# Attention with a computed bias: keys and values loaded between the first groups of bias rows, and the later rows shifted where they are written to memory

## The chip, the cores and the metric

One core of one Trainium2 chip. The metric is the device time of one execution in microseconds (us), median of three runs.

## What is computed

Two batches, eight heads, 576 positions, head dimension 64, all in float32. The scores are the scaled products of queries and keys plus a bias that a small network computes from the distance of two positions; then a softmax, the product with the values, and two feed-forward blocks on the 1152 x 512 result.

```
scores = scale * np.matmul(q, k.transpose(0, 1, 3, 2))
psi_rel = np.log1p(np.abs(rel));  psi_i = np.log1p(np.maximum(pos[:, None], 1.0))
h = np.maximum((psi_rel / psi_i)[..., None] @ w1 + b1, 0.0)
scores = scores + (h @ w2).transpose(2, 0, 1)[None]
attn = softmax(scores);  x = np.matmul(attn, v)
x = swiglu_block(rms_norm(x));  out = (s * relu(x @ w_in) ** 2 + b) @ w_out
```

## The kernel before

The order of the work is written out by hand: each engine, and each engine's queue of transfers, runs its instructions in program order. SP (SyncE) issues all transfers named here. A transfer that it issues waits on SP for its data, and holds up those behind it.

**Bias.** The 576 query positions are cut into 36 groups of 16 (`g`), each with 16 x 8 heads = 128 rows. `hidden(g)` (L169) makes four tiles `hq`, one for each quad of queries, mostly on VectorE (L182), the third of some early groups on ScalarE (L178), the fourth on GpSimd from group 12 on. `bias_mm(g)` multiplies them with `w2` (L202), `bias_out(g)` (L206) moves the result out of PSUM into a tile `br` (four buffers), on ScalarE (L221), for group 20 on VectorE (L219). For groups 0 to 7 the row has all 576 columns already, and one transfer puts the 128 rows into the bias tile of chunk 0 (L229, `bias<-br`): partition 8 i + g of it takes query i's eight heads. From group 8 on a row has 591 columns, is the same for all 16 queries but for a shift, and makes a detour: it is written to DRAM as it stands (L225, `rows<-br`, row pitch 592), and `bias_in(g)` (L231) reads it back with another start for each query (L239, `bias<-rows`):

```
src = bass.AP(tensor=r.tensor, offset=r.offset + 15, ap=[[H * RW - 1, 16], [RW, H], [1, S]])
```

A chunk of bias is 128 queries, made of eight groups; two chunk buffers are in use. The last chunk has 64 queries, each group of it read back twice.

**Attention.** A unit `u` is a pair of heads of a tile of 128 queries (four units to a tile, the first four with batch 0, the next four with batch 1; 36 units). `scores_mm(u)` (L261) needs q of the tile and k number u % 8; `soft(u, e)` (L273, VectorE) adds the bias chunk, finds the extreme for the softmax and frees the PSUM bank of the scores; `expo` (L280, ScalarE); `turn_mm` (L289, L291) transposes, `turn_out` (L298) copies; `values_mm` (L339) needs v number u % 8. `finish_*` normalise a finished tile: `finish_n` (L380, `x`), `finish_c` (L386).

**The schedule.** Stage -2 makes groups 0 to 7, `hide(g + LEAD)` behind each (`groups`, L503). The loop `for s in range(-2, PAIRED)` then takes one unit a step: loads, group s + 11 (stage -1: groups 8 to 10 behind the first scores), `bias_in`, scores and `soft` of unit s + 1, `values_mm` of unit s - 1. In it k number s + 3 is loaded in steps -1 to 4, and v number s + 1 in steps 0 to 6; k 0, k 1 and v 0 come ahead of everything. From s = 8 on the loop `for s in range(PAIRED, NU + 2, 2)` takes two units a step, with `hide(s + 13)` and `hide(s + 14)` behind the second `expo`. All behind unit 35 (feed-forward blocks, weights split on ScalarE, VectorE and GpSimd) is untouched by the change.

Of the kernel before, what the change touches and what calls it, by code (L numbers as in the profile page):

```python
# [8 lines left out]
F32 = mybir.dt.float32  # L9
# [8 lines left out]
P = 128  # L18
B, H, S, D = 2, 8, 576, 64
# [10 lines left out]
NJ = 3  # L30
TJ = NT // NJ
RW = S + 16
NEAR = S + P
TILES = list(range(NTT))
POOL_QUAD = 3
# [10 lines left out]
PAIRED = 8  # L46
# [6 lines left out]
def tile_kernel(ctx: ExitStack, tc: tile.TileContext, q, k, v, ltab, lg, cst, cst2, rms_g, wg, wv, wo, win, wo2, s_p, b_p, out):  # L53
    nc = tc.nc
    ctx.enter_context(tc.manual_schedule())

    def pool(stack, name, bufs, side="left", space=None):
        kw = {"space": space} if space else {}
        return stack.enter_context(tc.tile_pool(name=name, bufs=bufs, side=side, reuse_waits="tile", **kw))
# [32 lines left out]
    dram = pool(att, "dram", 1, space=bass.MemoryType.DRAM)  # L92
# [4 lines left out]

    near = tab_p.tile([P, NEAR], F32, name="near")
    tab = tab_p.tile([P, S], F32, name="tab")
# [6 lines left out]
    cb = ac.tile([P, 2], F32, name="cb")  # L106
    spot = ac.tile([P, 1], F32, name="spot")
    owed = []
    g_row = tab_p.tile([1, DM + P], F32, name="g_row")
    mh = const.tile([P, 1], F32, name="mh")  # L110
    g_bc = const.tile([P, DM], F32, name="g_bc")
# [23 lines left out]
    def load_k(n):  # L135
        ks[n] = ac.tile([P, S], F32, name=f"ks{n}")
        nc.sync.dma_start(out=ks[n], in_=k[:, n])

    def load_v(n):
        t = ac.tile([P, 10, D], F32, name=f"vs{n}")  # L140
        nc.sync.dma_start(out=t, in_=v[:, n])
        vs[n] = t
# [21 lines left out]
    rows = {}  # L164

    def reach(g):
        return S if g < 8 else max(16 * g + 15, S - 1 - 16 * g) + 1

    def hidden(g, owed):  # L169
        hms[g] = []  # L170
        d = reach(g)
        for tq in range(4):
            n = 4 * g + tq
            hq = h_p.tile([P, S], F32, name="hq")[:, :d]
            src = near[:, P - 1 - 4 * n:P - 1 - 4 * n + S] if g < 8 else tab[:, :d]
            hms[g].append(hq)
            if tq == ACT_QUAD and g in ACT_EARLY:
                nc.scalar.activation(hq, src, AF.Relu, bias=nthr[:, n:n + 1], scale=w1_sb)  # L178
                continue

            def go(eng, hq=hq, src=src, n=n):
                eng.tensor_scalar(hq, src, w1_sb, thr[:, n:n + 1], op0=ALU.mult, op1=ALU.max)  # L182

            if tq != POOL_QUAD or g < POOL_FROM:
                go(nc.vector)
            elif owed is None:
                go(nc.gpsimd)
            else:
                owed.append(lambda go=go: go(nc.gpsimd))
# [16 lines left out]
    def bias_out(g, pb):  # L206
        left = 0 if g < 8 else 16 * g + 15
        br = br_p.tile([P, RW], F32, name="br")
        to = left + S - (16 * g if left else 0)
        if left:  # L210
            parts = [(br[:, left:to], pb[0][:, :to - left])]
            for f, bank in enumerate(pb):
                a, b = max(512 * f, 1), min(512 * f + 511, left)
                parts.append((br[:, left - b:left - a + 1], bank[:, b - 512 * f:(a - 512 * f - 1) if a > 512 * f else None:-1]))
        else:
            parts = [(br[:, :to], pb[:, :to])]
        for dst, src in parts:
            if g == PAIRED + 12:
                nc.vector.tensor_scalar(dst, src, minv_sb[:, g:g + 1], cb[:, 0:1], op0=ALU.mult, op1=ALU.add)  # L219
                continue  # L220
            nc.scalar.activation(dst, src, AF.Identity, bias=cb[:, 1:2] if g in ACT_EARLY else cb[:, 0:1],  # L221
                                 scale=minv_sb[:, g:g + 1])
        if left:
            rows[g] = dram.tile([P, RW], F32, name=f"rows{g}")
            nc.sync.dma_start(out=rows[g][:, :to], in_=br[:, :to])  # L225
        else:
            if 0 not in bias:
                bias[0] = bias_p.tile([P, H, S], F32, name="bias")
            nc.sync.dma_start(out=bias[0][g:P:8, :, :], in_=br[:, :to])  # L229

    def bias_in(g):  # L231
        qc, g16 = divmod(g, 8)
        if qc not in bias:
            bias[qc] = bias_p.tile([P, H, S], F32, name="bias")
        r = rows.pop(g)
        src = bass.AP(tensor=r.tensor, offset=r.offset + 15, ap=[[H * RW - 1, 16], [RW, H], [1, S]])
        for dst in ([0] if qc < 4 else [0, 64]):
            to = dst + (P if qc < 4 else D)
            nc.sync.dma_start(out=bias[qc][dst + g16:to:8 if qc < 4 else 4, :, :], in_=src)  # L239
# [25 lines left out]
    def soft(u, e, ps):  # L265
        if u % 4 == 0 and e == 0:
            sums[u // 4] = st_p.tile([P, H], F32, name="rs")
        if e == 0:
            prs[u] = pr_p.tile([P, 2 * S], F32, name="pr")
        h = 2 * (u % 4) + e  # L270
        sn = sn_p.tile([P, S], F32, name="sn")
        nm = st_p.tile([P, 1], F32, name="nm")
        nc.vector.tensor_tensor_reduce(out=sn, in0=ps, in1=bias[chunk(u)][:, h, :],  # L273
                                       scale=-1.0 / SCALE, scalar=3.0e38, op0=ALU.add, op1=ALU.min, accum_out=nm)
        sns[u, e] = sn, nm
# [179 lines left out]
    for g in range(AHD, NG):  # L455
        plan[g - 11 if g > 10 else -1].append(g)

    def hide(g, owed=None):
        if g < NG:
            hidden(g, owed)  # L460

    def s_view(i):
        return reg[:, :16 * TJ].rearrange("p (s i c t) -> p s i c t", s=4, i=2, c=2)[:, :, i]
# [34 lines left out]
    for g in range(LEAD):  # L498
        hide(g)
        if g == 0:  # L500
            nc.scalar.activation(cb[:, 0:1], pcb[:, 0:1], AF.Copy, scale=SCALE)
            nc.scalar.activation(cb[:, 1:2], pcb[:, 0:1], AF.Copy, scale=m_sb)
    def groups(s):  # L503
        for g in plan[s]:
            pb = bias_mm(g)
            bias_out(g, pb)
            if s == -1 and g == AHD:
                hide(11)
            if s == -2:
                hide(g + LEAD)  # L510

    for s in range(-2, PAIRED):
        r = s % 4
        if s >= 5 and r == 1:
            finish_a(s // 4 - 1)
        if s >= 0 and r == 0:
            load_q(s // 4 + 1)
        if -1 <= s < 5:
            load_k(s + 3)
        if 0 <= s < 7:  # L520
            load_v(s + 1)
        landed = list(rows)[:2 if s > 3 else 1]
        if s != -1:
            groups(s)
        for g in landed:
            bias_in(g)
        if s >= 6 and r == 2:
            finish_b(s // 4 - 1)
        if 0 <= s + 1 < NU:
            ps = scores_mm(s + 1)  # L530
            if s == -1:
                groups(s)
                nc.tensor.matmul(pg, g_row[:, DM:], g_row[:, :DM], start=True, stop=True)
            soft(s + 1, 0, ps[0])
        if 0 <= s < NU:
            turn_out(s, 0, turn_mm(s, 0))
        if s == 7:
            finish_n(0)
        if 0 <= s + 1 < NU:
            expo(s + 1, 0)  # L540
            soft(s + 1, 1, ps[1])
        if 0 <= s < NU:
            for e in (1, 2):
                turn_out(s, e, turn_mm(s, e))
        if 0 <= s + 1 < NU:
            expo(s + 1, 1)
        if s == 0:
            nc.scalar.copy(g_bc, pg)
        if s >= 6 and r == 2:
            finish_s(s // 4 - 1)  # L550
        if s >= -1:
            hide(s + 13)
        if s == 4:
            nc.sync.dma_start(out=s_sb, in_=s_p)
            nc.sync.dma_start(out=b_sb, in_=b_p)
        if 0 <= s - 1 < NU:
            values_mm(s - 1)
        if s >= 5 and r == 1:
            finish_t(s // 4 - 1)
        if s == 6:  # L560
            xs = [act_p.tile([P, NKC, NT], F32R, name=f"xs{i}", tag=f"x{i}") for i in range(2)]
        if s >= 7 and r == 3:
            finish_c(s // 4 - 1)
# [10 lines left out]
    for s in range(PAIRED, NU + 2, 2):  # L574
# [6 lines left out]
        if s + 1 < NU:  # L581
            ps = scores_mm(s + 1)
            for e in range(2):
                soft(s + 1, e, ps[e])
            if s % 4 == 2:
                finish_s(s // 4 - 1)
        for d in range(2):
            if s - 2 + d > PAIRED - 2:
                values_mm(s - 2 + d)
            if s + 1 < NU:  # L590
                expo(s + 1, d)
            if d and tile_ends:
                finish_a(s // 4 - 1)
            if d:
                hide(s + 13, owed)
                hide(s + 14, owed)
            groups(s + d)
        if s in BITS:
            part = bits_of(BITS[s])
# [431 lines left out]
def _layout(inputs):  # L1031
# [20 lines left out]
    mg = np.log1p(np.maximum(pos.astype(np.float32), np.float32(1.0)))  # L1052
    x = np.arange(NEAR)[None, :] - (P - 1) - np.arange(4)[:, None]
    ltab = np.repeat(lg[np.minimum(np.abs(x), S - 1)], HID, axis=0)
# [57 lines left out]
```

## Time and profile before

| | us |
|---|---|
| median of 3 runs | 596.91 (596.03 to 598.53) |
| the profiled execution's own time | 597.67 |
| its span, first to last instruction | 595.7 |
| TensorE (PE) busy | 587.0 |
| VectorE (DVE) busy | 441.7 |
| ScalarE (ACT) busy | 337.8 |
| GpSimd (POOL) busy | 239.1 |

Times in the rows are us from the start of the span, unless marked ns. PE is TensorE's matmul and PEld its weight load; SPq is SP's queue of issues. A matmul's end is modelled, so a busy PE may be waiting inside; the idle time in brackets, with what ended it, tells more. The DMA share is the mean busy share of the core's 16 DMA engines.

### The profile page before, as it was taken

To read this page: it belongs to the slowest core of one execution; us is meant where nothing else is said; L and a number is where in the kernel's file an instruction comes from. 1 tells how busy PE (TensorE), PEld (TensorE's weight loads), DVE (VectorE), ACT (ScalarE), POOL (GpSimd) and SP (SyncE) were. 2 spreads that over 40 slices of the span, in tenths; PEclk is the share of its full clock that TensorE was granted. 3 is DMA by queue.
4 is the path that set the end of the run, shared out by engine and by line. 5 is a ranking of instruction groups with operands and counts; after the bars stand their busy time and mean duration, and the time that the engine had idled before them with its cause. 6 is when DMAs were issued, how large, how long until landed. Compare 5 with 4: busy or idle time off the path is not lost.

```text
span 595.7 us, 13412 instructions
## 1 busy us (share of the span) xinstructions
PE 587.0 (99%) x5366; PEld 529.9 (89%) x5366; DVE 441.7 (74%) x789; ACT 337.8 (57%) x678; POOL 239.1 (40%) x222
## 2 busy tenths in 40 slices
PE   9999899999999999999999999999999999999997
PEld 5466666667789999999999999999999999999996
DVE  7977989977776887788787944559995336999541
ACT  8887688887775555555656432246662235665110
POOL 0522255450566655655644432323333233333320
PEclk9999999999999999999999999999999999999999
DMA  7898446475012232233223222212222322222321
GB/s 207 260 301 247 154 141 180 142 233 136 24 53 72 72 111 102 72 104 109 72 73 106 84 95 106 89 54 95 83 72 106 107 72 70 72 100 78 127 87 53
DMA packets 25743, 67.26 MB, mean 113 GB/s; under 512 B 3121, under 2 KB 4689, under 8 KB 25682
## 3 DMA queue, kind: packets, MB, share of 16 engines
q1 hardware_dynamic: 25634, 66.40, 34.7%
q8 instruction: 42, 0.69, 0.5%
q14 instruction: 19, 0.16, 0.1%
q10 hardware_dynamic: 48, 0.02, 0.0%
HBM read 53.21 MB, written 10.83 MB: 108 GB/s over the span
## 4 chain that ended last, share of the span: by engine, by line
PE 86%; DMA 5%; DVE 3%; ACT 3%; POOL 1%; issue 1%; SPq 0%; DVEq 0%; ACTq 0%; POOLq 0%
PE c L736 11%; PE c L712 8%; PE c L713 8%; PE c L711 8%; PE b L736 7%; PE po L339 6%; PE b L712 6%; PE b L713 6%; PE b L711 6%; PE a L261 5%; PE b L289 4%; DMA vs<-in_v 3%; PE b L202 3%; PE po L712 2%; PE po L713 2%; PE po L711 2%
## 5 line engine op out<-in xcount | busy, mean ns | idle before, releaser
L447 POOL TENSOR_TENSOR wlo<-wa,whi 128x512 fp32r<-128x512 f32 (+1 forms) x71 | 95.7, 1351 | 75.1 <-ACT whi L444 75.1
L421 POOL TENSOR_SCALAR wa<-wa 128x512 f32<-128x512 f32 x68 | 47.6, 700 | 125.4 <-ACT wa L420 123.1
L273 DVE CUSTOM_DVE_ANT_0 sn<-a,bias 128x576 f32<-128x576 f32 x72 | 51.6, 753 | 16.5 <-PE a L261 8.2
L280 ACT ACTIVATE pr<-sn,nm 128x576 f32<-128x576 f32 x72 | 56.6, 788 | 12.4 <-DVE nm L273 12.4
L420 ACT ACTIVATE wa<-wraw 128x512 f32<-128x512 f32 x68 | 45.9, 676 | 31.1 <-DMA wraw<-in_wo 28.0
L444 ACT CAST whi<-wa 128x512 fp32r<-128x512 f32 x68 | 42.0, 617 | 23.1 <-DVE wa L432 22.9
L182 POOL TENSOR_SCALAR hq<-tab,c_sb,thr 128x384 f32<-128x384 f32 (+17 forms) x24 | 43.5, 1819 | 28.7 <-PE b L202 28.7
L429 DVE TENSOR_SCALAR wa<-wa 128x512 int32<-128x512 int32 x46 | 28.8, 625 | 31.5 <-POOL wa L421 31.5
L712 PE MATMUL c<-f,whi 128*128 128x384 f32 (+1 forms) x150 | 49.7, 331 | 0.0
L713 PE MATMUL c<-f,wlo 128*128 128x384 f32 (+1 forms) x150 | 49.7, 331 | 0.0
L711 PE MATMUL c<-f,whi 128*128 128x384 f32 (+1 forms) x150 | 49.7, 331 | 0.0
L736 PE MATMUL c<-xs,whi 128*128 128x384 f32 x184 | 46.8, 335 | 0.0
L261 PE MATMUL a<-ks,q 64*64 64x352 f32 (+1 forms) x576 | 44.6, 415 | 0.2 <-ACT br L221 0.2
L969 DVE SCALAR_TENSOR_TENSOR f<-hv,b_sb,f 128x384 fp32r<-128x384 f32 x48 | 40.8, 854 | 1.9 <-ACT f L968 1.8
L339 PE MATMUL po<-pt,vs 128*32 128x128 f32 (+1 forms) x1344 | 41.0, 264 | 0.0
L339 PEld LDWEIGHTS po<-pt,vs 128*32 128x32 f32 x1344 | 33.2, 110 | 8.8 <-issue 8.3
L965 DVE SCALAR_TENSOR_TENSOR hv<-sg,s_sb 128x384 f32<-128x384 f32 x48 | 36.4, 758 | 5.9 <-ACT sg L964 5.9
L289 PE MATMUL b<-ident,pr 128*128 128x128 f32 x288 | 39.3, 279 | 1.1 <-DVE br L219 1.1
L261 PEld LDWEIGHTS a<-ks,q 64*64 64x64 f32 x576 | 19.3, 132 | 23.1 <-issue 5.3
L792 POOL TENSOR_TENSOR tl<-ut,th 128x512 fp32r<-128x512 f32 x20 | 25.9, 1296 | 33.4 <-ACT th L791 21.8
L289 PEld LDWEIGHTS b<-ident,pr 128*128 128x128 f32 x288 | 30.8, 141 | 9.3 <-issue 7.7
L736 PE MATMUL b<-xs,whi 128*128 128x384 f32 x152 | 38.7, 335 | 0.0
(201 smaller groups left out, 1649.4 us busy)
## 6 DMA issues: line engine op xcount, KB each, us to landing
wraw<-in_wo SPq DMA_DIRECT2D x28, 512.0 KB, 3.5
bias<-rows SPq DMA_DIRECT2D x32, 288.0 KB, 4.6
rows<-br SPq DMA_DIRECT2D x28, 295.5 KB, 3.1
wraw<-in_win SPq DMA_DIRECT2D x16, 512.0 KB, 3.5
wraw<-in_wg SPq DMA_DIRECT2D x12, 512.0 KB, 3.5
wraw<-in_wv SPq DMA_DIRECT2D x12, 512.0 KB, 3.9
vs<-in_v SPq DMA_DIRECT2D x8, 320.0 KB, 6.6
ks<-in_k SPq DMA_DIRECT2D x8, 288.0 KB, 6.7
```

The source lines that it names most:

```text
L261: nc.tensor.matmul(ps[e][qc, f], qt[u // 4][ed, hp, qc], ks[b[i % len(b)] * NP + hp][ed, f], start=True, stop=True, tile_position=(e * D, ...
L273: nc.vector.tensor_tensor_reduce(out=sn, in0=ps, in1=bias[chunk(u)][:, h, :], scale=-1.0 / SCALE, scalar=3.0e38, op0=ALU.add, op1=ALU.min, ...
L280: nc.scalar.activation(prs[u][:, e * S:(e + 1) * S], sn, AF.Exp, bias=nm, scale=-1.0, accum_out=sums[u // 4][:, h:h + 1])
L289: nc.tensor.transpose(pT[:, c * P:(c + 1) * P], pr[:, o:o + P], ident)
L339: nc.tensor.matmul(dst, w, a, start=c == 0, stop=c == NQC - 1, tile_position=(0, o))
L420: nc.scalar.activation(a.bitcast(F32), raw[:, :, 1].bitcast(F32), AF.Abs)
L421: nc.gpsimd.tensor_scalar(a.bitcast(F32), a.bitcast(F32), F64_MAX, F64_MIN, op0=ALU.min, op1=ALU.max)
L447: nc.gpsimd.tensor_tensor(out=lo[:, c:c + step], in0=w[:, c:c + step].bitcast(F32), in1=hi[:, c:c + step].bitcast(F32), op=ALU.subtract)
L711: nc.tensor.matmul(ps, hi[:, ws], ah, start=first, stop=False)
L712: nc.tensor.matmul(ps, hi[:, ws], al, start=False, stop=False)
L713: nc.tensor.matmul(ps, lo[:, ws], ah, start=False, stop=last)
L736: nc.tensor.matmul(ps, w[i][:, (c0 + c) * P:(c0 + c + 1) * P], a[h][c], start=first and c == 0 and i == 0 and h == 0, stop=c == 1 and i == ...
```

## The change

Three parts. (1) Three k and three v loads move from the unit loop to stage -2, one behind each of groups 0 to 5, and the rest come one a step. (2) The rows of groups 8 to 35 are written to DRAM shifted by one element per query (pitch 608), and read back with one start for all. (3) The three VectorE passes of group 22 are kept back from the end of the `expo` in step s = 8 and made in step 10 behind `soft` of unit 11.

```
+DW = S + 32
+    kept = []
-    def hidden(g, owed):
+    def hidden(g, owed, kept=None):
             if tq != POOL_QUAD or g < POOL_FROM:
-                go(nc.vector)
+                go(nc.vector) if kept is None else kept.append(lambda go=go: go(nc.vector))
         if left:
-            rows[g] = dram.tile([P, RW], F32, name=f"rows{g}")
-            nc.sync.dma_start(out=rows[g][:, :to], in_=br[:, :to])
+            rows[g] = dram.tile([P, DW], F32, name=f"rows{g}")
+            r = rows[g]
+            nc.sync.dma_start(out=bass.AP(tensor=r.tensor, offset=r.offset + 1, ap=[[H * DW + 1, 16], [DW, H], [1, to]]),
+                              in_=br[:, :to])
-        src = bass.AP(tensor=r.tensor, offset=r.offset + 15, ap=[[H * RW - 1, 16], [RW, H], [1, S]])
+        src = r.rearrange("(i h) w -> i h w", h=H)[:, :, 16:16 + S]
+    EARLY = [[x] for x in ((load_k, 2), (load_v, 1), (load_k, 3), (load_v, 2), (load_k, 4), (load_v, 3))] + [[], []]
+    LOADS = {-1: [(load_k, 5)], 0: [(load_v, 4)], 1: [(load_k, 6)], 2: [(load_v, 5)], 3: [(load_k, 7)],
+             4: [(load_v, 6)], 5: [(load_v, 7)]}
             if s == -2:
                 hide(g + LEAD)
+                for fn, n in EARLY[g]:
+                    fn(n)
-        if -1 <= s < 5:
-            load_k(s + 3)
-        if 0 <= s < 7:
-            load_v(s + 1)
+        for fn, n in LOADS.get(s, ()):
+            fn(n)
                 soft(s + 1, e, ps[e])
+            while kept:
+                kept.pop(0)()
-                hide(s + 14, owed)
+                hide(s + 14, owed, kept if s == PAIRED else None)
```

## Rows read from the trace of the kernel before

**Rows 1.** The page: busy time, share of the span and instructions of each engine.

```profile
PE 587.0 (99%) x5366; PEld 529.9 (89%) x5366; DVE 441.7 (74%) x789; ACT 337.8 (57%) x678; POOL 239.1 (40%) x222
```

**Rows 2.** Chain that ended last, in order of time: start, length, what.

```profile
26.24 0.33 SPq L225
...
27.96 8.01 DMA vs<-in_v
...
51.58 4.67 DMA rows<-br
```

**Rows 3.** Stretches: length, busy PE, PEld, DVE, ACT, POOL, clock, DMA share, GB/s.

```profile
7.00:8.20 1.20, 1.20 (x17) 0.47 (x14) 1.20 (x3) 1.20 (x3) 0.00 (x0) 1.00 0.97 360
8.30:20.00 11.70, 11.46 (x123) 5.40 (x124) 11.70 (x27) 9.61 (x13) 0.00 (x0) 1.00 0.71 197
...
30.00:46.00 16.00, 16.00 (x290) 10.67 (x291) 11.85 (x31) 13.54 (x33) 4.19 (x3) 1.00 1.04 310
...
53.00:58.00 5.00, 3.63 (x67) 2.61 (x68) 2.11 (x6) 3.04 (x8) 3.16 (x3) 1.00 0.90 263
58.00:68.00 10.00, 8.50 (x119) 5.72 (x122) 9.96 (x27) 6.58 (x16) 1.99 (x3) 1.00 0.54 158
```

**Rows 4.** Timeline at the first `soft`: start, length, instructions [idle before <- releaser].

```profile
22.60 0.76 DVE L273 CUSTOM_DVE_ANT_0 sn<-a,bias 128x576 f32<-128x576 f32 x1 [0.17 <-DMA bias<-br]
22.94 0.88 PE L202 MATMUL b<-hq,c_sb 128*32 128x400 f32 x8
...
23.75 0.19 PEld L261 LDWEIGHTS a<-ks,q 64*64 64x64 f32 x4 [0.65 <-DVE nm L273]
```

**Rows 5.** Timeline at the first `soft` of chunk 1 (unit 8).

```profile
49.23 1.31 SPq L239 DMA_DIRECT2D bias<-rows  x2
...
56.27 0.76 DVE L273 CUSTOM_DVE_ANT_0 sn<-a,bias 128x576 f32<-128x576 f32 x1 [2.89 <-DMA rows<-br]
...
57.85 0.63 PE L386 MATMUL b<-ident,x 128*128 128x128 f32 x4 [1.37 <-DVE x L380]
```

**Rows 6.** Timeline of the first paired step (s = 8).

```profile
61.94 2.34 DVE L182 TENSOR_SCALAR hq<-tab,c_sb,thr 128x352 f32<-128x352 f32 x6
...
65.42 0.63 PE L289 MATMUL b<-ident,pr 128*128 128x128 f32 x4 [1.14 <-DVE br L219]
...
67.28 0.44 PE L316 MATMUL b<-ident,pr 128*128 128x128 f32 x2 [0.36 <-DVE pt L298]
```

**Rows 7.** DMA issues: out<-in, queue, count, KB each, median us from issue to landing.

```profile
bias<-rows SPq DMA_DIRECT2D x32, 288.0 KB, 4.6
rows<-br SPq DMA_DIRECT2D x28, 295.5 KB, 3.1
...
vs<-in_v SPq DMA_DIRECT2D x8, 320.0 KB, 6.6
ks<-in_k SPq DMA_DIRECT2D x8, 288.0 KB, 6.7
...
bias<-br SPq DMA_DIRECT2D x8, 288.0 KB, 3.4
```

**Rows 8.** SP's issues in stage -2, and line 229 alone (ns min/median/max).

```profile
8.26 10.72 SPq L229 DMA_DIRECT2D bias<-br  x8
19.02 0.58 SPq L137 DMA_DIRECT2D ks<-in_k  x1
...
L229 SPq DMA_DIRECT2D bias<-br x8: 536/537/647, 8.3 to 18.4; - x8
```

**Rows 9.** Timeline: scores of two units that follow one another.

```profile
36.08 1.20 PE L261 MATMUL a<-ks,q 64*64 64x352 f32 x16
...
40.14 1.20 PE L261 MATMUL a<-ks,q 64*64 64x352 f32 x16
```

**Rows 10.** Timeline of the second paired step (s = 10): scores of unit 13.

```profile
76.17 1.20 PE L261 MATMUL a<-ks,q 64*64 64x352 f32 x16
76.28 0.69 DVE L390 TENSOR_TENSOR xs<-b,xs 128x512 fp32r<-128x512 f32 x1 [0.84 <-ACT xs L389]
```

More of the change, by code (lines that the diff above doesn't have):

```diff
@@ L456, in tile_kernel, with hide @@
         plan[g - 11 if g > 10 else -1].append(g)
-    def hide(g, owed=None):
+    def hide(g, owed=None, kept=None):
         if g < NG:
-            hidden(g, owed)
+            hidden(g, owed, kept)
     def s_view(i):
```

## The prediction

> **What bounds the kernel now.** I began with the page: TensorE is busy 99% of a span of 595.7 us [rows 1]. That share is no proof that every stage is TensorE's, so next came the chain of work that ended last, in order of time. The reader should see one odd piece in it [rows 2]: from 27.96 us on the chain runs through four transfers, one behind the other (the first 8.01 us, the last 4.67 us to 56.25), and leaves them at a `soft` of VectorE. Before and behind that stretch it is nearly all TensorE.
>
> Then the table by stretches [rows 3]. From 30 to 46 us the DMA engines are full (share 1.04, 310 GB/s). From 8.3 to 20 us, while the first eight groups of bias rows go out, they are not (0.71, 197 GB/s), and behind 58 us they are half idle. TensorE has no gap from 30 to 46 us; it has them from 53 to 58 (3.63 of 5.00 busy) and from 58 to 68 (8.50 of 10.00).
>
> So there are two places. **The first** is the start of the scores: VectorE's first `soft` began 0.17 us after it could have, held by the last of the eight bias transfers, and the weight load of the next unit's scores waited 0.65 us for that `soft` [rows 4]. **The second** is the change from one chunk of bias to the next: `soft` of unit 8 waited 2.89 us for a transfer, so `x` (L380) came late and TensorE stood 1.37 us [rows 5]. The row names rows<-br; `soft` reads the bias tile, whose last two transfers were issued from 49.23 us on, so it is the queue as a whole that was late. Behind it VectorE works without a gap and TensorE waits for it 1.14 and 0.36 us more [rows 6].
>
> **The change, part by part.**
>
> *Six loads between the first groups.* Behind the bias transfers of groups 0 to 5, SP now issues three k and three v loads: 3 x 288 + 3 x 320 KB [rows 7] = 1.87 MB. On SP this is six issues of up to about 0.6 us (0.58 for the k load at 19.02 [rows 8]); eight bias issues take 10.72 us from first to last, one each (10.72 - 0.54) / 7 = 1.45 us, of which an issue holds 0.54 [rows 8]. SP waits there for ACT's eviction anyway, so the issues cost nothing; without that cover they would cost 6 x 0.58 = 3.5 us. No load waits for anything, so no bias issue is held up by a wait.
>
> The transfers themselves are another matter: all go through one queue in order, and the last bias transfer, which the first `soft` needs, now stands behind 1.87 MB more. Where loads run alone (7.0 to 8.2 us: share 0.97, 360 GB/s [rows 3]) that is 1.87 / 0.36 = 5.2 us of queue. Upper bound of the delay: 5.2 us, if the idle share cannot be used. Lower bound: from 8.3 to 20 us the share is 0.71, so 0.29 x 11.7 = 3.4 us were free; 5.2 - 3.4 = 1.8 us. Between them the nearest row is the full stretch: a unit there lasts 40.14 - 36.08 = 4.06 us [rows 9] and carries one bias transfer, one of rows, one k and one v. The three plain ones (295.5 + 288 + 320 KB = 0.925 MB) take 2.57 us at 360 GB/s, which leaves 1.49 us for the bias transfer, as much as its whole slot of 1.45 us when it ran alone. So a bias transfer and a plain one add up, they do not overlap. I take 4.2 us, near the upper end. [...]
>
> What hangs on it: VectorE waits in order, so `hide(12)`, the second `soft` and all behind them wait too; scores of unit 1 need the PSUM bank that `soft` frees [rows 4]; ACT's exponentials follow. ACT's `br` ring of four buffers fills as well (a buffer is free when its transfer landed, 3.4 us after the issue now [rows 7], four slots of 1.45 us = 5.8 us later it is wanted), so groups 8 to 10 are evicted late, but still ahead of the delayed `soft`. From unit 2 to unit 8 TensorE sets the pace at 4.06 us and cannot catch up. The 4.2 us go straight into the end.
>
> *Fewer loads later.* Each step from unit -1 to 5 then issues one load where two stood. A unit needs about 4.06 - 0.82 = 3.2 us of queue in 4.06, so the backlog melts, and the last two transfers of chunk 1 land in about their median 4.6 us [rows 7] after an issue that SP no longer holds back. The wait of 2.89 us goes. Worth on TensorE: 1.37 us. Late next is VectorE itself, below.
>
> *Group 22's three VectorE passes moved.* They leave the run of six that takes 2.34 us at 61.94 (2.34 / 2 = 1.17 us) and go behind `soft` of unit 11. With VectorE ahead by most of the 2.89 us plus 1.17 us, the waits of 1.14 and 0.36 us [rows 6] go too. Bounds for wait and move together: below 1.4 us (only the first stall), above 1.37 + 1.14 + 0.36 = 2.9 us. Of this, about 0.6 us is paid back: the 1.17 us now stand ahead of `hide(23)`, `hide(24)` and the `soft` of unit 12, which frees the bank for the scores at 76.17; the first cover is VectorE's gap of 0.84 us behind that, and I count half of the 1.17 us as uncovered [rows 10]. Their reader, group 22's matmuls, comes after two `values`. I take 2.8 - 0.6 = 2.2 us.
>
> *Rows written shifted, read straight.* The 28 writes and 32 reads stay, of the same bytes. Reads at odd starts become even, writes the reverse; the issue of a write may take 0.54 us like a bias issue in place of 0.33 [rows 2, 8], covered by SP's waits. No row shows a write at an odd start. Below: reads 0.1 us cheaper each, worth nothing where the queue has slack. Above: a write costs double, 0.82 more per unit, 3.2 + 0.82 = 4.0 us of 4.06, just hidden. I take zero.
>
> **Sum:** + 4.2 - 1.4 - 0.8 = + 2.0 us. The profiled execution took 597.67 us, so 599.7 us on its account. It lies 0.76 us above the median of 596.91 us; for the median I forecast 598.9 us, 0.3% more. A difference under 0.5% (3.0 us) cannot be told from none here.
>
> **Rivals.** (a) *The idle share is used*: loads pass while bias packets wait, the delay is 1.8 us or less. [...] For it: 29% of the engines' time free from 8.3 to 20 us. Against: the additive slot [rows 9]. Net -0.4 us at 1.8, -2.2 us at none, 594.7 to 596.5 us; with all of the 2.9 us too it touches -3. It decides below 2.2 us of delay.
> (b) *Shifted writes are slow*, and the wait at unit 8 stays, now added to the late start: once a write holds the queue for over 0.82 + 0.86 = 1.7 us, a unit needs more than 4.06. Then only the move helps (about 0.7 us): + 3.5 us, 600.4 us. For it: 28 writes at odd 4-byte starts. Against: the reads at odd starts before ran inside a 1.49 us slot.
> (c) *TensorE cools.* Between group 11's matmuls (to 23.8 us [rows 4]) and the delayed scores of unit 1 it would stand some 4 us, against 1.37 us at unit 8 now [rows 5]. The granted clock is 1.00 in every row [rows 3]; no row shows what such a stand does to it. [...]
> (d) *It does not do what it says*: the wait at unit 8 stays for a reason other than the queue. Net + 3.5 us too.
>
> **How the numbers follow.** Forecast (delay 3 to 5 us, wait gone, net 0 to + 3): 0.55. Rival (a) 0.23, a third of it beyond -3 us with what I overlooked; (b) 0.08, (c) 0.09, (d) 0.05. Faster 0.08; slower 0.25 (b, c, d and a tail of 0.03 of the forecast); same 0.67. The range runs from inside (a), 595.2, to beyond (b), 602.0; left out are the ends of (a) and (c).
>
> **What would show it.** Right: the first `soft` at about 26.8 us with an idle of about 4 us put to bias<-br; DMA share near 1.0 from 10 to 25 us and below 0.9 behind 30; no wait of `soft` near unit 8; scores of unit 13 some 2 us later than 76.17. Wrong: a first `soft` within 1.5 us of 22.60 (rival a), a DMA wait left at the chunk's change (b, d), or a granted clock below 1.00 behind the first `soft` (c). rows<-br landing far over 3.1 us would put the shift in question.

## The result, and the profile after

Six runs of the changed kernel had a median of 604.06 us (602.49 to 604.61), six of the kernel before, on the same chip, 597.77 us (596.03 to 598.77). The ratio is 1.0103, with a 95% interval of 1.0082 to 1.0124: the change costs 1%, 6.3 us, twice what can be told from none here, and the time lies above the upper end of the range. The profiled execution took 604.35 us, its span is 602.3 us.

The page first: busy time by engine, then the granted clock and the busy share of the DMA engines in 40 slices of 15 us.

```profile
PE 589.5 (98%) x5366; PEld 529.8 (88%) x5366; DVE 442.7 (73%) x789; ACT 338.5 (56%) x678; POOL 237.7 (39%) x222
...
PEclk9879999999999999999999999999999999999999
DMA  7979555658013223313323232122323322222321
```

TensorE has 2.5 us more busy time than in [rows 1], with as many instructions: they ran slower somewhere. The second and third digits of the clock say where, from 15 to 45 us. The table of stretches opens these slices (columns as in [rows 3]).

```profile
10.00:25.00 15.00, 9.91 (x108) 3.51 (x112) 10.93 (x25) 8.50 (x13) 0.00 (x0) 0.93 1.04 264
17.00:22.00 5.00, 1.24 (x20) 0.47 (x16) 3.63 (x9) 1.87 (x3) 0.00 (x0) 1.00 1.05 272
22.00:23.00 1.00, 1.00 (x16) 0.37 (x15) 0.00 (x0) 0.41 (x1) 0.00 (x0) 0.99 1.02 210
23.00:26.00 3.00, 3.00 (x22) 0.85 (x24) 1.30 (x4) 1.08 (x2) 0.00 (x0) 0.50 1.06 234
29.00:30.00 1.00, 0.00 (x0) 0.00 (x0) 0.34 (x1) 0.89 (x2) 1.00 (x2) 0.90 0.80 260
30.00:36.00 6.00, 5.52 (x29) 3.13 (x33) 4.44 (x13) 4.17 (x11) 1.09 (x1) 0.50 0.78 224
36.40:46.00 9.60, 9.60 (x166) 5.97 (x162) 7.02 (x18) 8.22 (x21) 3.68 (x3) 0.99 0.76 203
```

From 10 to 25 us the DMA engines are full (1.04) and move only 264 GB/s. From 17 to 22 us TensorE was busy for only 1.24 of 5.00 us, and from 23 to 26 us it was granted 0.50 of its clock; so it was from 30 to 36 us. From 36.4 to 46 us, where [rows 3] had 1.04, the queue now has slack (0.76).

Next the timeline around the first `soft` (start, length, instructions, in brackets the idle time before and its releaser), which answers to [rows 4].

```profile
17.73 0.83 ACT L223 ACTIVATE br<-a,cb,c_sb 128x576 f32<-128x576 f32 x1 [1.68 <-DMA bias<-br]
...
18.61 0.81 PE L265 MATMUL a<-ks,q 64*64 64x352 f32 x4 [1.34 <-ACT br L223]
...
20.96 0.83 ACT L223 ACTIVATE br<-a,cb,c_sb 128x576 f32<-128x576 f32 x1 [2.40 <-DMA bias<-br]
...
21.84 1.19 PE L265 MATMUL a<-ks,q 64*64 64x352 f32 x12 [2.42 <-ACT br L223]
...
29.66 0.76 DVE L277 CUSTOM_DVE_ANT_0 sn<-a,bias 128x576 f32<-128x576 f32 x1 [3.27 <-DMA ks<-in_k]
...
30.48 2.12 PE L265 MATMUL a<-ks,q 64*64 64x352 f32 x10 [1.60 <-DVE nm L277]
```

The first `soft` starts at 29.66 us instead of 22.60. ACT runs out of `br` buffers (1.68 and 2.40 us of waiting for bias transfers to land), TensorE stands 1.34 and 2.42 us behind it, with 0.81 us of work between, and 1.60 us more ahead of unit 1's scores. The chain of waits goes the same way (start, length, what):

```profile
20.96 0.84 ACT br L223
21.81 0.54 SPq L233
22.40 7.17 DMA ks<-in_k
29.66 0.76 DVE sn L277
```

The row names the k load, the issue right behind the last bias transfer. `soft` of unit 0 does not read k 5, and k 5 landed 7.6 us after its issue, at 30.0 us, when `soft` had begun. What `soft` needs is the bias transfer issued at 21.81 us; it landed 7.6 us later too, at 29.4 us, and the experiments name it.

The DMA issues [rows 7] show what was traded (columns as there):

```profile
bias<-rows SPq DMA_DIRECT2D x32, 288.0 KB, 4.2
rows<-br SPq DMA_DIRECT2D x28, 295.5 KB, 3.5
...
vs<-in_v SPq DMA_DIRECT2D x8, 320.0 KB, 4.7
ks<-in_k SPq DMA_DIRECT2D x8, 288.0 KB, 5.0
...
bias<-br SPq DMA_DIRECT2D x8, 288.0 KB, 7.7
```

k and v land sooner after their issue, the eight direct bias transfers take 7.7 us where they took 3.4. Last the scores of single units, from the timeline: units 2, 3 and 8, the `soft` of unit 8, units 9, 11 and 13 [rows 5, 10].

```profile
36.76 1.20 PE L265 MATMUL a<-ks,q 64*64 64x352 f32 x16
...
40.87 1.20 PE L265 MATMUL a<-ks,q 64*64 64x352 f32 x16
...
61.78 1.20 PE L265 MATMUL a<-ks,q 64*64 64x352 f32 x16
...
63.11 0.76 DVE L277 CUSTOM_DVE_ANT_0 sn<-a,bias 128x576 f32<-128x576 f32 x1 [0.86 <-PE a L265]
...
65.86 1.20 PE L265 MATMUL a<-ks,q 64*64 64x352 f32 x16
...
73.51 1.20 PE L265 MATMUL a<-ks,q 64*64 64x352 f32 x16
...
82.67 1.24 PE L265 MATMUL a<-ks,q 64*64 64x352 f32 x16
```

The same scores before, units 2, 3, 8, 9 and 11:

```profile
27.52 1.20 PE L261 MATMUL a<-ks,q 64*64 64x352 f32 x16
...
32.00 1.20 PE L261 MATMUL a<-ks,q 64*64 64x352 f32 x16
...
52.91 1.20 PE L261 MATMUL a<-ks,q 64*64 64x352 f32 x16
...
58.40 1.21 PE L261 MATMUL a<-ks,q 64*64 64x352 f32 x16
...
67.65 1.20 PE L261 MATMUL a<-ks,q 64*64 64x352 f32 x16
```

This is the account of the 6.5 us, event by event:

| event | before | after | after - before |
|---|---|---|---|
| first `soft` (unit 0) | 22.60 | 29.66 | + 7.06 |
| scores, unit 1 | 23.75 | 30.48 | + 6.73 |
| scores, unit 2 | 27.52 | 36.76 | + 9.24 |
| scores, unit 3 | 32.00 | 40.87 | + 8.87 |
| scores, unit 8 | 52.91 | 61.78 | + 8.87 |
| scores, unit 9 | 58.40 | 65.86 | + 7.46 |
| scores, unit 11 | 67.65 | 73.51 | + 5.86 |
| scores, unit 13 | 76.17 | 82.67 | + 6.50 |
| scores, unit 35 | 166.96 | 173.50 | + 6.54 |

Lost: 7.06 us at the first `soft` and 1.81 more by unit 3. Nothing moves from unit 3 to unit 8. Won: 1.41 at the change of chunk, 1.60 at group 22, of which 0.64 is paid back by unit 13. Then nothing more happens.

### The profile page after: what moved, and what is told of

It is laid out like the page before. It is cut to its first block, busy times and chain, and to the rows that moved or that the text cites. A ratio compares the mean times of both kernels' runs of the same rounds, so it can differ in the third digit from the quotient of the medians.

```text
span 602.3 us, 13411 instructions
## 1 busy us (share of the span) xinstructions
PE 589.5 (98%) x5366; PEld 529.8 (88%) x5366; DVE 442.7 (73%) x789; ACT 338.5 (56%) x678; POOL 237.7 (39%) x222
## 4 chain that ended last, share of the span: by engine, by line
PE 88%; DVE 3%; DMA 3%; ACT 2%; issue 1%; POOL 1%; SPq 0%; DVEq 0%; ACTq 0%; POOLq 0%
PE c L746 11%; PE c L722 8%; PE c L723 8%; PE c L721 8%; PE b L746 7%; PE po L343 7%; PE a L265 6%; PE b L722 6%; PE b L723 6%; PE b L721 6%; PE b L293 5%; PE b L204 3%; PE po L722 2%; PE po L723 2%; PE po L721 2%
## 5 line engine op out<-in xcount | busy, mean ns | idle before, releaser
L184 POOL TENSOR_SCALAR hq<-tab,c_sb,thr 128x384 f32<-128x384 f32 (+17 forms) x24 | 42.0, 1757 | 38.9 <-PE b L204 38.9
L184 DVE TENSOR_SCALAR hq<-tab,c_sb,thr 128x448 f32<-128x448 f32 (+17 forms) x87 | 37.6, 496 | 4.1 <-PE b L204 4.1
```

## The experiments

The theory: the six loads ahead of the last bias transfer fill the queue, that sets the first `soft`, and everything behind follows. The rivals: the `br` ring of four, the clock, the shifted writes. Each ratio is to the kernel before, run on the same chip.

**Parts alone and one part undone.** The early loads put back, shift and group 22 kept:

```
-                for fn, n in EARLY[g]:
-                    fn(n)
...
-        for fn, n in LOADS.get(s, ()):
-            fn(n)
+        if -1 <= s < 5:
+            load_k(s + 3)
+        if 0 <= s < 7:
+            load_v(s + 1)
```

> The changed kernel with the k and v loads at their old places; the shifted rows and the moved passes of group 22 stay. Theory (the early loads cost the whole loss, by the queue they share with the bias transfers): first soft back at 22.6 us (29.66 in the changed kernel), granted clock 1.00 throughout, the wait of about 2.9 us at soft of unit 8 back, and only group 22's move left over: 0.7 to 1.0 us under the kernel before, ratio about 0.998 to 1.000. Rival (the shifted writes share in the loss, 28 of them): the run stays 1 us or more above the kernel before, and rows<-br lands later than 3.1 us with a longer wait at unit 8 than 2.89 us.

598.87 against 597.55 us, ratio 1.0015 (0.9991 to 1.0039): the loss of 6.3 us is gone. But 0.7 to 1.0 us under the kernel before were expected, and the run lies 1.3 us over it, as its rival, the shifted writes, would have it; they are tried alone below. The timeline has the first `soft` back, and the wait at unit 8 as well:

```profile
22.45 0.76 DVE L277 CUSTOM_DVE_ANT_0 sn<-a,bias 128x576 f32<-128x576 f32 x1
...
57.51 0.76 DVE L277 CUSTOM_DVE_ANT_0 sn<-a,bias 128x576 f32<-128x576 f32 x1 [3.55 <-DMA rows<-br]
```

The converse is the kernel before with the early loads as its only change (`EARLY`, the `LOADS` of the diff and their two loops; rows and group 22 as before):

> The kernel before with nothing but the six loads between the bias transfers (and one load a step later). Theory (this part makes the whole loss; the shift is hidden behind a queue with slack, and the moved passes give 0.8 to 1.7 us): first soft near 29.7, scores of units 3 to 8 at a constant 8 to 9.5 us behind the kernel before, no wait at unit 8, time 7 to 8.5 us over it, ratio 1.012 to 1.015, above the changed kernel. Rival (the shift costs the changed kernel 1.6 us as it does alone, ratio 1.0027): ratio 1.009 to 1.011, at or under the changed kernel.

605.72 against 597.56 us, 1.0135 (1.0118 to 1.0153). The timeline at the first `soft` names the transfer that it reads:

```profile
30.20 0.76 DVE L273 CUSTOM_DVE_ANT_0 sn<-a,bias 128x576 f32<-128x576 f32 x1 [2.98 <-DMA bias<-br]
```

So the early loads alone cost 8.2 us. The other two parts, each alone on the kernel before. The shift, that is the new destination and source (`RW` to `DW`):

```
+            nc.sync.dma_start(out=bass.AP(tensor=r.tensor, offset=r.offset + 1, ap=[[H * DW + 1, 16], [DW, H], [1, to]]),
+                              in_=br[:, :to])
...
+        src = r.rearrange("(i h) w -> i h w", h=H)[:, :, 16:16 + S]
```

> The kernel before with nothing but the shifted writes and straight reads. Theory, formed on the run with the loads at their old places (there rows<-br landed in 3.7 us, 3.1 before, and soft of unit 8 waited 3.55 us, 2.89 before): the shift makes the write slower, in a queue that is full from 25 to 55 us, so unit 8 waits 0.5 to 1.2 us longer and the time is 0.5 to 2.5 us over the kernel before. Rival (my zero): rows<-br lands in 3.1 us, unit 8 starts at 52.9, and the time is that of the kernel before within 0.5 us.

599.18 against 598.08 us, 1.0027 (1.0010 to 1.0043). A row of its DMA issues, and the stretch from 30 to 46 us in its table:

```profile
rows<-br SPq DMA_DIRECT2D x28, 295.5 KB, 3.7
```

```profile
30.00:46.00 16.00, 15.01 (x276) 10.10 (x280) 11.46 (x30) 12.78 (x32) 4.18 (x3) 1.00 1.05 299
```

In a queue that is full (1.05) the shift is not free: TensorE, without a gap from 30 to 46 us before [rows 3], stands 1.0 us here. From unit 3 to unit 6 its scores take 13.37 us, and 12.82 in the run with the loads back; in the four profiles with rows as before and loads at their old places (the kernel before three times, group 22 alone) they take 12.17 or 12.18. What stands between the shift and TensorE is not shown. The landing is no proof: the median went from 3.1 to 3.7 us, but with rows written as before it was 3.6 us with group 22 alone and 4.2 in the last run below. Group 22 alone:

```
-                hide(s + 14, owed)
+                hide(s + 14, owed, kept if s == PAIRED else None)
```

> The kernel before with nothing but group 22's three passes moved. Theory (they are worth 1.2 to 1.6 us at unit 11 and give 0.5 to 0.7 us back at unit 13, as the changed kernel's starts of the scores say): unit 11 about 1.3 us earlier than the kernel before against unit 10, unit 13 0.6 to 1.0 us earlier than 76.17, time 0.6 to 1.0 us under the kernel before, which may not show over the scatter. Rival: with the wait at unit 8 still there VectorE is late anyway, and unit 13 starts at 76.0 to 76.3.

596.82 against 598.08 us, 0.9972 (0.9958 to 0.9986): the part that wins. By its timeline unit 11's scores follow unit 10's after 4.21 us, 5.77 before. Units 8 and 9 stand out:

```profile
53.27 1.20 PE L262 MATMUL a<-ks,q 64*64 64x352 f32 x16
54.79 0.76 DVE L274 CUSTOM_DVE_ANT_0 sn<-a,bias 128x576 f32<-128x576 f32 x1 [1.05 <-DMA rows<-br]
...
57.36 1.20 PE L262 MATMUL a<-ks,q 64*64 64x352 f32 x16
```

The loads stand where they stood, and yet TensorE loses nothing at unit 8: 57.36 - 53.27 = 4.09 us, against 5.49 in the profile of before. So the kernel before was profiled twice more, unchanged:

> The kernel before, word for word, once more, for its profile alone. Group 22's move by itself cannot touch anything ahead of unit 8, yet its profile had no wait at unit 8 (57.35 - 53.27 = 4.08 us from unit 8 to 9, against 5.49). Theory (the wait stands on the border: the queue is full from 25 to 55 us and whether it ends late differs by execution): the wait at soft of unit 8 differs by over 1 us between looks, between none and 3 us. Rival (it is in every execution of the kernel before): 2.4 to 3.4 us again.

> The same once more: a third profile of the kernel before. Theory as for the second look: wait at unit 8 anywhere between none and 3 us. Rival: 2.4 to 3.4 us.

`soft` of unit 8 in the one (599.80 us) and in the other (599.94 us):

```profile
58.20 0.76 DVE L273 CUSTOM_DVE_ANT_0 sn<-a,bias 128x576 f32<-128x576 f32 x1 [4.62 <-DMA rows<-br]
```

```profile
58.42 0.76 DVE L273 CUSTOM_DVE_ANT_0 sn<-a,bias 128x576 f32<-128x576 f32 x1 [4.31 <-DMA rows<-br]
```

The same program waits 2.89, 4.62 or 4.31 us there, and unit 9 follows unit 8 after 5.49, 7.23 or 6.91 us. The wait that the change removes is no constant; what it is worth in the median of before stays open between nothing and some 3 us. The clock takes part in it: in these two executions TensorE stood 2.52 and 2.79 us there, 1.37 in the first [rows 5], and behind that it was granted 0.66 of its clock, 1.00 in the first [rows 3]. The stretch of the first of the two:

```profile
60.00:65.00 5.00, 5.00 (x72) 2.90 (x74) 5.00 (x15) 2.99 (x8) 0.00 (x0) 0.66 0.70 177
```

Unit 10 then followed unit 9 after 5.10 us (3.48 in the first execution), and unit 11 followed unit 10 after 4.15 (5.77): in this place the slow clock cost nothing that stayed.

**Which property of the early loads.** The ring of `br` buffers doubled in the changed kernel:

```
-    br_p = ring(gen, "br", 4)
+    br_p = ring(gen, "br", 8)
```

> The changed kernel with eight br buffers in place of four, so that ScalarE's evictions of groups 6 to 10 no longer wait for a bias transfer to land (5.5 us of such waits in the changed kernel), and the last bias transfer is issued near 19 us, not 21.8. Theory (the queue is full from 10 to 29 us, the ring only fills behind it): first soft within 0.7 us of 29.66, time within 0.2% of the changed kernel. Rival (the ring of four is what makes the start late): first soft 2 to 3 us earlier, about 27 us, and 2 to 3 us off the time.

604.00 us, 1.0103 (1.0057 to 1.0150): nothing. ACT no longer waits; VectorE waits instead, in one piece and for the bias transfer:

```profile
30.05 0.76 DVE L277 CUSTOM_DVE_ANT_0 sn<-a,bias 128x576 f32<-128x576 f32 x1 [7.75 <-DMA bias<-br]
```

The ring was a place to wait, not the cause. TensorE's standing is one piece here too, 7.02 us ahead of unit 1's scores, and from 30 to 36 us it was granted 0.61 of its clock. Next the same six loads, issued in a row behind group 7, so that no bias transfer stands behind them:

```
-                for fn, n in EARLY[g]:
-                    fn(n)
...
-    LOADS = {-1: [(load_k, 5)], 0: [(load_v, 4)],
+    LOADS = {-1: [(load_k, 2), (load_v, 1), (load_k, 3), (load_v, 2), (load_k, 4), (load_v, 3), (load_k, 5)], 0: [(load_v, 4)],
```

> The changed kernel with the same six loads issued in one row behind the last of the eight bias transfers, ahead of k 5, instead of between them. Theory (what costs is the place ahead of the last bias transfer): first soft back at 22.6 to 23.3 us, no clock loss, and the gain behind stays (wait at unit 8 gone or smaller, since the idle queue between 20 and 26 us is used): 1.5 to 2.5 us under the kernel before, ratio 0.996 to 0.998. Rival (the bytes cost wherever they are put in the first 30 us): the rows of groups 8 to 10 and the second q come late, a later unit waits, and the time is that of the kernel before or above.

596.83 against 597.55 us, 0.9987 (0.9965 to 1.0009): the loss is gone, but the gain of 1.5 to 2.5 us that was expected is not shown. From its timeline:

```profile
23.26 0.76 DVE L277 CUSTOM_DVE_ANT_0 sn<-a,bias 128x576 f32<-128x576 f32 x1 [0.37 <-DMA bias<-br]
...
30.07 1.09 ACT L223 ACTIVATE br<-b,cb,c_sb 128x384 f32<-128x384 f32 x2 [0.75 <-DMA rows<-br]
```

So the order in the queue is what costs. With the loads behind, the ring does cost a little: ACT waits 0.75 us for a `br` buffer, and unit 3 follows unit 2 after 5.32 us, 4.48 before and 4.47 in the last run below, with a ring of eight. And with two of the six left early (k 2 and v 1), four behind group 7:

> The changed kernel with only two of the six loads (k 2, v 1) between the bias transfers of groups 0 to 2, and the other four behind group 7. Theory (each early load costs its own queue time, about 1.0 to 1.2 us, less what the idle share takes at first): first soft 1.0 to 2.2 us later than with none (22.45 and 23.26 us in the two runs without), that is 23.7 to 25.2 us, granted clock 1.00, time 1 to 2 us over the run with all six behind group 7, about that of the kernel before. Rival (the delay comes only once the queue is so long that transfers stand for sems or buffers): first soft within 0.5 us of 23.0.

598.23 against 598.08 us, 1.0010 (0.9994 to 1.0025).

```profile
24.76 0.76 DVE L277 CUSTOM_DVE_ANT_0 sn<-a,bias 128x576 f32<-128x576 f32 x1
```

With none early the first `soft` starts at 23.26, with two at 24.76, with six at 29.66: 0.75 us for each of the first two, (29.66 - 24.76) / 4 = 1.2 us for each of the rest. With two, `soft` itself waits for no transfer (the row has no brackets): VectorE was late by 1.90 us of waiting for TensorE, which stood behind ACT, and ACT had waited 2.53 us for a `br` buffer. So here the delay came by way of the ring.

**The clock.** Idle 128x128 matmuls (`keep_clock`, L154) where TensorE stood: eight between the two heads of unit 0's first scores, six behind the `g_row` product, six behind group 11.

```
+                if u == 0 and e == 0 and f.start == 0:
+                    keep_clock(8)
...
+        if s == 0:
+            keep_clock(6)
...
+                keep_clock(6)
```

> The changed kernel with 20 idle 128x128 matmuls (results never read) put where TensorE stands: eight between the two heads of the first scores, six behind group 10, six behind group 11. Theory (the 2.1 to 2.5 us that unit 2 loses more than unit 1 come from the granted clock of 0.50 from 23 to 26 and from 29.8 to 36.4 us): clock 1.00 through the start, first soft unchanged near 29.7, scores of unit 2 at about 34.5 in place of 36.76, and 2 us off the time, ratio to the kernel before about 1.007. Rival (that stretch is bound by VectorE and the queue, not by the clock): unit 2 stays near 36.8 and the time within 0.5 us of the changed kernel.

604.26 us, 1.0101 (1.0055 to 1.0148). The stretch from 30 to 35 us, and unit 1's scores in the timeline:

```profile
30.00:35.00 5.00, 5.00 (x49) 3.28 (x48) 4.01 (x10) 3.48 (x9) 2.60 (x2) 1.00 0.79 230
```

```profile
32.69 1.20 PE L265 MATMUL a<-ks,q 64*64 64x352 f32 x16
```

The clock is full here (it had been 0.66 from 20 to 25 us all the same), and unit 2 follows unit 1 after 3.25 us in place of 6.28 (35.94 - 32.69). But unit 1 itself starts 2.2 us later, behind the idle matmuls, and the 2 us that the clock was expected to give back do not show in the time. A second placing (six ahead of the first scores, eight between, three and three behind) did not part the two either:

> The changed kernel with 20 idle matmuls, results never read, placed so that they end before their successors' data is there: six ahead of the first scores, eight between their two heads, three behind group 10, three behind group 11. Theory (in the first trial the idle matmuls stood in front of unit 1's scores and cost 1.7 us of what the clock gave back): clock 1.00 behind 25 us, scores of unit 1 at 30.5 to 31, of unit 2 at 33.8 to 34.7 in place of 36.76, and 1.5 to 2.5 us under the changed kernel. Rival (the clock has no part in it): unit 2 at 36 us or later with the clock at 1.00, and the changed kernel's time.

604.26 against 597.56 us, 1.0108 (1.0086 to 1.0130). Three of its idle matmuls, in the timeline, came too late themselves, for want of a PSUM bank, and the clock fell again behind that stand (0.66 from 30 to 35 us):

```profile
31.01 1.41 PE L157 MATMUL b<-ident 128*128 128x128 f32 x6 [2.27 <-ACT br L223]
```

**What follows from it all.** Loads behind group 7, a ring of eight, group 22's passes moved, rows written and read as before:

```
+    LOADS = {-1: [(load_k, 2), (load_v, 1), (load_k, 3), (load_v, 2), (load_k, 4), (load_v, 3), (load_k, 5)],
+             0: [(load_v, 4)], 1: [(load_k, 6)], 2: [(load_v, 5)], 3: [(load_k, 7)], 4: [(load_v, 6)], 5: [(load_v, 7)]}
...
-    br_p = ring(gen, "br", 4)
+    br_p = ring(gen, "br", 8)
...
-                hide(s + 14, owed)
+                hide(s + 14, owed, kept if s == PAIRED else None)
```

> Put together from what helped: the kernel before, without the shift, with the six loads in one row behind the last bias transfer, eight br buffers and group 22's passes moved. Theory (loads use the queue's idle time behind 20 us, no stall of ScalarE for a br buffer at 30 us, no wait at unit 8): first soft at 22.4 to 23.3, unit 8 at 52.9 to 53.5 without a wait, 2 to 3 us under the kernel before, ratio 0.995 to 0.997, and under both kernels. Rival (the queue is as full at 50 us as before, since all bytes are still to be moved by then): a wait of over 1 us at unit 8 stays and the ratio is 0.998 or more.

596.13 against 598.08 us, 0.9955 (0.9942 to 0.9969): faster than both kernels. Its timeline has the early `soft` and no DMA wait at unit 8:

```profile
23.08 0.76 DVE L274 CUSTOM_DVE_ANT_0 sn<-a,bias 128x576 f32<-128x576 f32 x1 [0.39 <-DMA bias<-br]
...
55.04 0.76 DVE L274 CUSTOM_DVE_ANT_0 sn<-a,bias 128x576 f32<-128x576 f32 x1 [1.38 <-PE b L290]
```

Against group 22 alone (0.9972) the intervals overlap, so what the loads behind group 7 add to it is not shown by the medians; its five runs do lie closer together, 595.68 to 596.41 us.

## Why the prediction failed, step by step

**The early loads: the step that failed, by the size of its term.** The mechanism came as written: SP's issues hidden, bias transfers held up in the one queue, VectorE waiting in order, and, from unit 3 to unit 8, no catching up. But the step put the delay at 4.2 us and no higher than 5.2; it measured 7.06. Both numbers came from 360 GB/s, which [rows 3] shows for plain loads that run alone. The queue that the loads were put into was one of scattered bias transfers. These are the stretches from the first bias issue to the landing of the last bias transfer, before and after (columns as in [rows 3]):

```profile
8.30:22.60 14.30, 14.06 (x141) 6.29 (x139) 14.13 (x32) 11.53 (x17) 1.12 (x1) 1.00 0.71 199
```

```profile
8.30:29.40 21.10, 15.13 (x151) 4.85 (x146) 14.02 (x31) 12.79 (x20) 3.06 (x2) 0.92 0.96 239
```

14.3 us at a share of 0.71 are 10.2 us of busy DMA engines, 21.1 us at 0.96 are 20.3. So the engines were busy for 10.1 us more, and moved 2.2 MB more (239 GB/s x 21.1 us less 199 GB/s x 14.3 us: the six loads and a part of the rows behind them). That is 217 GB/s, where 360 had been counted. The idle share was used: 14.3 x 0.29 = 4.1 us were idle before, 21.1 x 0.04 = 0.8 after. The 10.1 us less these 3.3 are the 6.8 us by which the stretch grew. The upper bound was no bound, because the added bytes cost the engines some two thirds more than plain loads alone had shown. Why they take longer in this mix is open. The slot of 1.45 us, which led the step to 4.2, was no price of a bias transfer either: VectorE was busy 11.70 of 11.70 us there, and the queue 0.71 [rows 3]. Rival (a), by which the idle share is used and the delay stays small, is refuted in the delay: with the early loads alone, with the ring of eight and in the changed kernel the first `soft` was 7.1 to 7.6 us late.

**TensorE's clock, rival (c), came true in part.** At 0.09 it was underrated. No row of the kernel before shows what a stand does to the clock, or how far beyond the range it would carry (c); the changed kernel shows 0.50. TensorE did not stand 4 us in one piece but 1.34 and 2.42 us, almost together, and later 1.60 us, and was granted 0.50 of its clock behind both places (23 to 26 and 30 to 36 us). Unit 2's scores follow unit 1's after 36.76 - 30.48 = 6.28 us, nearly all of it at 0.50, against 27.52 - 23.75 = 3.77 before at 1.00. Part of that is made up by other waits that went, and what is left is the + 1.81 us between the first `soft` and unit 3. The clock's exact share stays open: with the idle matmuls the way from the first `soft` to unit 3 took 40.42 - 30.16 = 10.26 us, against 40.87 - 29.66 = 11.21 in the changed kernel, but the idle matmuls are in it, and the total did not move. The greater part of the loss was the queue, + 7.06 us at the first `soft`.

**The `br` ring** did fill, as the step said, but "still ahead of the delayed `soft`" was only nearly right: the last bias issue came at 21.81 instead of 18.4 us. It made no difference, as the ring of eight shows.

**The wait at unit 8** went: 1.41 us on TensorE, 1.37 predicted. That the two agree is luck of the execution: in the other two of the kernel before, unit 9 came 1.74 and 1.42 us later still behind unit 8, which the step could not see from one profile.

**Group 22** gave 1.60 and took back 0.64, and with the wait of unit 8 the gains come to 1.41 + 1.60 - 0.64 = 2.37 us, 2.2 predicted. Alone it is worth 0.28%, so here the trace of one execution was a fair guide.

**The shift at zero** held where it was applied: from unit 3 to unit 8 the distance to before stays 8.87 us, where the queue has slack (share 0.89 from 40.87 to 61.78 us). Alone, in the full queue (1.05), it costs 0.27%. The medians of the parts point the same way: early loads and group 22 alone make 8.2 - 1.3 = + 6.9 us, and with the shift, which alone costs 1.1, the whole change still comes to + 6.3, not 8.0; their intervals, about 1 us to either side each, do not part the two for certain. SP's issue of a shifted write takes 0.53 us (0.54 predicted).

The sum with measured terms is 7.06 + 1.81 - 2.37 = + 6.5 us, and the spans differ by 602.3 - 595.7 = 6.6.

## What to carry to other kernels

Put a load behind the last transfer that the next consumer waits for, not between them: in one in-order queue six loads ahead of it cost 7 us here, though the engines looked a third idle (share 0.71), and behind it nothing that can be measured (ratio 0.9987). Do not price added bytes at the rate of the best neighbour: among the bias transfers these took some two thirds more of the engines' time (217 GB/s, 360 alone). And when a wait is worth one or two us, read it in several executions before counting on it.

## What was not expected of the hardware

- A queue of bias transfers and plain loads at a share of 1.04 moved 264 GB/s; plain loads alone 360 at 0.97 [rows 3]. A direct bias transfer writes 16 partitions that lie eight apart; whether that slows the queue is not shown: the slot of 1.45 us [rows 8] was the pace of VectorE, which had no gap, with the queue at 0.71, and in the changed kernel the last two of these transfers landed 0.7 us apart (18.58 + 10.1 and 21.81 + 7.6 us).
- `soft` of unit 8 waited between 1.05 and 4.62 us in four executions of kernels that do the same work up to there (before three times, and group 22 alone), and TensorE lost between nothing and 3 us by it. The DMA share from 25 to 55 us was 1.02 to 1.04 in all four, so the share does not tell how late the queue is. The GB/s of the same stretch do: 312, 294, 285 and 284 with waits of 1.05, 2.89, 4.31 and 4.62 us.
- TensorE was granted 0.50 from 23 to 26 us although it was busy in all of that stretch and in the microsecond ahead of it, at a clock of 0.99; the stand of 2.42 us had ended at 21.84. The fall shows behind the stand, in work that looks innocent; ahead of it, from 17 to 22 us, TensorE was busy for 1.24 of 5.00 us.
